# Loads in another order, w1 and w2 by halves of their columns: an attention and feed-forward kernel on one Trainium2 core

## The chip, the cores and the metric

The kernel runs on one core of a Trainium2 chip. The metric is the device time of one execution in microseconds. A core has several engines that run side by side, each through its own list of instructions in order: PE (the matmul engine, TensorE), DVE (VectorE), ACT (ScalarE), POOL (GpSimd) and SP (SyncE, which here only issues transfers). Transfers between the main memory and the core's SBUF are issued by SP or ACT (the hardware queues) or by POOL (the software queue) and are carried by 16 DMA engines. Matmuls write to PSUM, which here is one tile of eight banks; DVE or ACT must carry each result out of it.

## The reference

Attention with RMS-normalised q and k over 8 batches of 12 heads, 448 positions and 64 elements a head, and behind it a multiplicative feed-forward part on 3584 tokens of 768:

```python
def rmsnorm(x, g):
    rms = np.sqrt(np.mean(x * x, axis=-1, keepdims=True) + 1e-06)
    return x / rms * g
q_n, k_n = (rmsnorm(q, g_q), rmsnorm(k, g_k))
scores = 1.0 / np.sqrt(q.shape[-1]) * np.matmul(q_n, k_n.transpose(0, 1, 3, 2))
attn = softmax(scores)                      # over the last axis
x = np.matmul(attn, v)                      # then heads side by side: 3584 x 768
# feed-forward: w1, w2 768 x 1024; w3 1024 x 1024; w_out 1024 x 768
a = x @ w1
b = x @ w2
out = (a * b @ w3) @ w_out
```

All inputs and the output are float32. The kernel computes in bfloat16 with float32 sums.

## The kernel before

The work is cut into 24 quads: quad i holds four heads of one batch (three quads a batch). A quad passes through these steps:

1. **Load** of q and k (`load_qk`), 0.92 MB of float32, into one of three pairs of buffers, and of v (`load_v`), turned to bfloat16 on the way.
2. **Prep**: squares on ACT (`prep_sq`, L335), their sums on DVE (`prep_red`, L344), 1/rms on ACT as exp(-0.5 ln) (`prep_alpha`, L357 and L360), scaling on DVE (`prep_scale`, L376 to L390), and the transpose to the layout that the score matmuls need: on PE for the first five quads (L425), by a DMA transpose for the others (L402).
3. **Scores**: nine score units a quad, each eight matmuls (L457) into two banks and one exp on ACT (L471). Units go to PE in groups of three ("bursts", 24 matmuls).
4. **P x V**: three sets a quad, each 16 matmuls (L487): the sums of the rows with a matrix of ones, then the two halves of v. ACT makes 1/sum (L500, L502), DVE multiplies (L510) into xT.
5. When a batch's three quads are done, its **feed-forward** pieces go on a list of fillers (`push_ffn`): for each of eight column blocks x @ w1 (carried out to a_sb) and x @ w2 (multiplied by a_sb, L589), and the output matmuls of finished tokens (all on L523).

w3 @ w_out is computed first, on the core: each of the eight chunks of w3 is transposed on PE (L539), and 16 units of eight matmuls (L551) make w34 = w3 @ w_out, so that the feed-forward part ends with one product in place of two.

```python
    def w3_transpose(fc):
        ps, z = take(1)
        ...
        for gc in range(CF):
            nc.tensor.transpose(ps[:, gc, :], w3s[:, fc, gc * 128 : (gc + 1) * 128], ident)
        run("PE", 0.5)
        w3T_at[fc] = copy_out(z, w3T[:, :, fc * 128 : (fc + 1) * 128], ps, W_EV, CF * 128, True)

    def w34_unit(fc, nh):
        ...
        for gc in range(CF):
            nc.tensor.matmul(out=ps[:, 0:NH], lhsT=w3T[:, gc, fc * 128 : (fc + 1) * 128],
                             rhs=w_outs[:, gc, nh * NH : (nh + 1) * NH], ...)
        run("PE", 1.4)
        copy_out(z, w34s[:, fc, nh * NH : (nh + 1) * NH], ps[:, 0:NH], W_EV, NH)
```

The order of instructions on each engine is fixed when the program is built. The builder keeps a planned time for each engine (`clk`) with estimated costs, and a table of planned landing times (`LAND`); these planning values only decide an order, and nothing of them is in the program. In a first stage it takes, over and over, whatever PE can do first by the plan; where the plan sees a gap on PE it puts in matmuls on a constant tile (`warm`, L658), whose results are not read:

```python
        def choices():
            res = []
            m = burst_size()
            ...            # 0: a burst of score units; 1: a transpose of q and k
            ...            # 2: a P x V set
            if w34q:       # 3: the next of the w3 transposes and w3 x w_out units, in their order
                res.append((w34q[0][0](), 3, lambda: w34q.pop(0)[1]()))
            return res
        ...
        while w34q or not fillers:
            res = choices()
            ...
            x = min((x for x in res if x[0] <= now + 0.1), key=lambda x: x[1])
            gap = now - clk["PE"]
            if gap > 0.5 and now < 30:
                warm(int(gap * WARM_GAP / 0.22))
            clk["PE"] = now
            x[2]()
            try_load()
            try_v()
```

After it comes a steady stage, counted in score units: every third unit a burst of three, P x V sets at fixed distances from a quad's last burst (`KIND`), loads of q and k for quad n at unit 9 n + `LOAD_AT`, and the fillers spread over the rest. What remains of the fillers after the last quad is done at the end, with PE alone.

The loads of the first stage, in the old order:

```python
    LOADS = ["o0", "w0", "w1", "w2", "v0", "w3", "w4", "w5", "v1", "w6", "w7", "o1", "v2"]
    ...                    # o: a half of w_out's columns, w: a chunk of w3, v: a quad's v
        for t, part, eng, h0 in (             # quad 0, on SP's and ACT's queues
            (0, 0, nc.sync, 0), (1, 0, nc.scalar, 0), (1, 1, nc.sync, 0),
            (0, 0, nc.sync, 2), (1, 0, nc.scalar, 2), (1, 1, nc.scalar, 2),
        ):
            load_part(0, t, h0, 2, parts_of(0, t)[part], eng)
        ...
        load_qk(1)                            # on SP's queue
        load_qk(2)
        make_identity(nc, ident)
        if GATE is not None:                  # the software queue waits for quad 0's first q
            nc.gpsimd.tensor_copy(
                out=gate[0:NP0], in_=st[0][GATE[0]][0:NP0, GATE[1], 0, 0:1]
            )
        for x in LOADS:                       # on POOL's queue
            load_any(x)
        for h in range(HQ):
            for half in range(2):
                for w, src in ((w1s, moe_w1), (w2s, moe_w2)):
                    load_w12(w, src, h, half)
        load_v(3)
        warm(WARM)
```

Quads 3 and on are loaded on SP's queue as soon as their buffers may be written (`try_load`), on which the output's stores (L629) and the DMA transposes go as well.

## Time and profile before

| | |
|---|---|
| time, median of three runs | 378.12 us (378.03 to 378.63) |
| span of the profiled execution | 377.4 us |
| read from main memory, written to it | 46.66 MB, 11.01 MB |
| bytes moved by the DMA engines | 56.43 MB, mean 150 GB/s |
| score matmuls (L457) | 44.4 us of PE |
| P x V matmuls (L487) | 79.9 us of PE, four rows together |
| feed-forward matmuls (L523) | 245.5 us of PE, three rows together |
| w3 x w_out (L551) | 22.8 us of PE |

In a row of the groups stand the line, the engine and operation, what is written from what, the shape and the number; after the bar the busy time and the mean duration of one in ns, and after the second bar the time that the engine stood idle just before such instructions, with what ended it. A row of the waits has who waited for whom, the sum in us, how often, and the longest. A row of a timeline or of the chain starts with the start in us and the duration; consecutive instructions of one kind are one row. The window rows give the busy time and the number of instructions of each engine in a stretch, then the granted share of PE's clock, the busy share of the 16 DMA engines (as the trace counts it, it can read above 1) and the rate. Ends of matmuls are modelled, so neighbouring rows of PE can overlap by some tenths of a microsecond.

### The profile page before, as it was taken

The numbers are of one execution on the slowest core, as the hardware profiler recorded it, in microseconds if no ns is written. First come the engines' busy times: TensorE is split into PE (matmuls) and PEld (weight loads), VectorE is DVE, ScalarE is ACT, GpSimd is POOL, SyncE is SP. The second block draws the span as 40 slices with busy tenths as digits, with TensorE's granted clock in tenths as the row PEclk, the third lists the DMA queues.
The fourth block names the chain that finished last, engine by engine and source line by source line (L and its number), as shares of the span: only waits on it lengthen the run. The fifth ranks groups of instructions, "written<-read, shape, count | busy, mean of one in ns | idle before, by whom it ended". The sixth has DMA issues, their size and how long they took to land.

```text
span 377.4 us, 17123 instructions
## 1 busy us (share of the span) xinstructions
PE 364.8 (97%) x7677; PEld 197.7 (52%) x7678; DVE 239.9 (64%) x425; ACT 280.3 (74%) x472; POOL 76.6 (20%) x133
## 2 busy tenths in 40 slices
PE   5989999999999999999999998999999999999995
PEld 2346555555555565555555554555545555556563
DVE  5688898878676776687568656678668755321210
ACT  3779768889969888878798885988798887752222
POOL 7145454422022022022202211210201200000000
PEclk9899999999999999999999999999999999999999
DMA  8999999775989798958896989777996883004005
GB/s 178 236 232 230 226 215 215 92 142 118 195 180 167 151 147 177 213 81 187 159 197 107 157 184 180 158 120 161 196 176 86 199 150 61 2 20 113 2 20 152
DMA packets 92777, 56.43 MB, mean 150 GB/s; under 512 B 56928, under 2 KB 86688, under 8 KB 92704
## 3 DMA queue, kind: packets, MB, share of 16 engines
q1 hardware_dynamic: 70096, 42.45, 53.3%
q0 software_dynamic: 22016, 12.33, 24.4%
q8 instruction: 60, 0.98, 1.1%
q10 hardware_dynamic: 592, 0.56, 0.6%
q14 instruction: 13, 0.11, 0.1%
HBM read 46.66 MB, written 11.01 MB: 153 GB/s over the span
## 4 chain that ended last, share of the span: by engine, by line
PE 85%; DMA 8%; ACT 3%; SPq 1%; issue 1%; DVE 0%; ACTq 0%; DVEq 0%
PE banks_ps L523 54%; PE banks_ps L487 15%; PE banks_ps L457 9%; DMA k_sb<-in_k_dram 5%; PE banks_ps L551 5%; DMA q_sb<-in_q_dram 3%; ACT P L471 1%; PE banks_ps L425 1%; PE banks_ps L539 1%; ACT a_sb L203 1%; SPq L629 1%; SPq L254 1%; ACT sq L335 0%; ACT o_sb L203 0%; DVE o_sb L205 0%
## 5 line engine op out<-in xcount | busy, mean ns | idle before, releaser
L471 ACT ACTIVATE P<-banks_ps 128x896 bf16<-128x896 f32 x144 | 124.2, 922 | 14.0 <-PE banks_ps L457 13.7
L523 PE MATMUL banks_ps<-xT,w2s 128*32 128x448 bf16 x1536 | 83.8, 352 | 1.8 <-ACT a_sb L203 1.8
L523 PE MATMUL banks_ps<-xT,w1s 128*32 128x448 bf16 x1536 | 83.9, 353 | 0.0
L286 POOL DMA_DIRECT2D v_sb<-in_v_dram x72 | 43.8, 622 | 189.8 <-PE banks_ps L487 182.9
L523 PE MATMUL banks_ps<-w34s,abT 128*32 128x384 bf16 x1792 | 77.8, 326 | 0.0
L344 DVE TENSOR_REDUCE ssq<-sq 128x8 f32<-128x512 f32 (+1 forms) x96 | 63.5, 679 | 13.9 <-ACT sq L335 13.3
L589 DVE TENSOR_TENSOR abT<-banks_ps,a_sb 128x448 bf16<-128x448 f32 x64 | 39.8, 622 | 41.8 <-PE banks_ps L523 41.5
L523 PEld LDWEIGHTS <-abT 128*32 128x32 bf16 x1792 | 47.8, 97 | 26.5 <-DVE abT L589 0.3
L523 PEld LDWEIGHTS <-w2s 128*32 128x32 bf16 x1536 | 41.5, 97 | 33.4 <-issue 2.7
L523 PEld LDWEIGHTS <-w1s 128*32 128x32 bf16 x1536 | 40.8, 97 | 31.9 <-issue 2.2
L510 DVE TENSOR_TENSOR xT<-banks_ps,r 128x448 bf16<-128x448 f32 x48 | 29.6, 622 | 29.6 <-PE banks_ps L487 20.8
L203 ACT CAST a_sb<-banks_ps 128x448 bf16<-128x448 f32 x53 | 28.1, 530 | 25.9 <-PE banks_ps L523 25.1
L457 PE MATMUL banks_ps<-qkT 64*32 64x448 bf16 x1344 | 44.4, 357 | 0.7 <-DVE abT L589 0.3
L376 DVE TENSOR_TENSOR qtmp<-q_sb,alpha 128x512 bf16<-128x512 f32 (+1 forms) x48 | 33.0, 687 | 11.8 <-ACT alpha L360 10.3
L203 ACT COPY o_sb<-banks_ps 128x384 f32<-128x384 f32 x42 | 20.1, 478 | 23.1 <-PE banks_ps L523 23.0
L487 PE MATMUL banks_ps<-P,v_sb 128*32 128x448 bf16 x576 | 35.8, 354 | 0.0
L335 ACT ACTIVATE sq<-q_sb 128x512 f32<-128x512 f32 (+1 forms) x48 | 30.0, 625 | 5.6 <-DMA q_sb<-in_q_dram 5.6
L390 DVE TENSOR_TENSOR qks<-k_sb,alpha 128x512 bf16<-128x512 f32 x48 | 32.8, 684 | 0.6 <-ACT alpha L360 0.6
L335 ACT ACTIVATE sq<-k_sb 128x512 f32<-128x512 f32 x48 | 30.1, 628 | 3.2 <-DMA k_sb<-in_k_dram 3.2
L487 PEld LDWEIGHTS <-v_sb 128*32 128x32 bf16 x768 | 18.9, 96 | 18.7 <-issue 6.9
L457 PEld LDWEIGHTS <-qkT 64*32 64x32 bf16 x1344 | 15.1, 90 | 25.9 <-issue 21.0
L471 ACT ACTIVATE Pr<-banks_ps 128x896 bf16<-128x896 f32 x24 | 22.1, 920 | 2.2 <-PE banks_ps L457 2.2
(53 smaller groups left out, 265.3 us busy)
## 6 DMA issues: line engine op xcount, KB each, us to landing
out_dram<-o_sb SPq DMA_DIRECT2D x48, 192.0 KB, 2.9
k_sb<-in_k_dram SPq DMA_DIRECT2D x23, 256.0 KB, 5.9
q_sb<-in_q_dram SPq DMA_DIRECT2D x21, 256.0 KB, 4.7
k_sb<-in_k_dram SPq DMA_DIRECT2D x23, 192.0 KB, 5.7
q_sb<-in_q_dram SPq DMA_DIRECT2D x21, 192.0 KB, 5.0
v_sb<-in_v_dram POOLq DMA_DIRECT2D x24, 96.0 KB, 3.4
w3s<-in_moe_w_dram POOLq DMA_DIRECT2D x8, 256.0 KB, 10.6
w_outs<-in_moe_w_out_dram POOLq DMA_DIRECT2D x4, 384.0 KB, 10.8
```

The costliest lines, as they stand in the source:

```text
L203: nc.scalar.copy(out=out, in_=in_)
L286: nc.gpsimd.dma_start(out=dst.rearrange("p h j d -> p h (j d)"), in_=part.rearrange("p h j d -> p h (j d)"),)
L335: nc.scalar.activation(out=s["sq", pr][0:n, t], in_=(s["q"], s["k"])[t][0:n, 2 * pr : 2 * pr + 2], func=AF.Square,)
L344: nc.vector.tensor_reduce(out=s["ssq"][0:n, t, 2 * pr : 2 * pr + 2, :], in_=s["sq", pr][0:n, t], axis=AX, op=ADD,)
L376: nc.vector.tensor_tensor(out=s["qtmp"][0:n].transpose([0, 2, 1, 3]), in0=s["q"][0:n, hs], in1=alpha[0:n, 0, hs].unsqueeze(3).broadcast_to ...
L390: nc.vector.tensor_tensor(out=s["qks", pr][:, 1].transpose([0, 2, 1, 3]), in0=s["k"][:, hs], in1=alpha[:, 1, hs].unsqueeze(3).broadcast_to ...
L457: nc.tensor.matmul(out=sc[c0 : c0 + 32, u, 0:S], lhsT=qkT[u * D : (u + 1) * D, pr, 1, k0 : k0 + 32], rhs=qkT[u * D : (u + 1) * D, pr, 0, 0:S],
L471: lambda: nc.scalar.activation(out=dst, in_=sc[:, :, 0:S], func=AF.Exp),
L487: nc.tensor.matmul(out=ps[h * HALF : (h + 1) * HALF, :], lhsT=w, rhs=s["P"][:, h, j, :] if j < NF else s["Pr"][:, h % 2, :], start=(j == 0 ...
L510: lambda e: nc.vector.tensor_tensor(out=xT[b][:, 2 * m + kind - 1, :], in0=ps, in1=s["r"], op=MULT),
L523: nc.tensor.matmul(out=ps[32 * h : 32 * h + 32, 0:n], lhsT=lhsT[:, 32 * h : 32 * h + 32], rhs=rhs, start=start, stop=stop, tile_position=( ...
L589: lambda e: nc.vector.tensor_tensor(out=abT[bp][:, fi, odd * S : (odd + 1) * S], in0=ps[:, 0:S], in1=a_sb, op=MULT,),
```

## The change

w1 and w2 are loaded in two halves of their columns, for all rows, in place of slices of 32 partitions with all columns, so that the first column blocks of the feed-forward part need only the first half; the first stage may now take feed-forward pieces as well, and runs until the second half is planned to have landed. Quads 1 and 2 leave SP's queue and stand in the list of the software queue, among the weights, in the order in which they are meant to be needed; the gate at that queue's head is gone. Loads of later quads are placed 6 score units earlier (`LOAD_AT` from -17 to -23). The planning constants and the landing table are set anew.

```diff
--- before.py
+++ after.py
@@ -52,32 +52,33 @@
     O_BUFS = 3
     F_BUFS = 3
     G = 3
-    KIND = (3, 4, 6)
+    KIND = (2, 4, 6)
     N_PE_T = 5
     N_SQ_ACT = 24
-    A_EV = "AD"
-    O_EV = "AD"
-    W_EV = "DA"
-    BIAS = 0.2
-    SLACK = (0.3, 0.3)
-    EXP_SLACK = 0.6
+    A_EV = 'AD'
+    O_EV = 'AD'
+    W_EV = 'DA'
+    BIAS = 0.6
+    SLACK = (0.5, 0.2)
+    EXP_SLACK = 1.05
     WARM = 16
-    WARM_GAP = 0.6
-    PACE = 0.8
-    SLACK_0 = (2,1)
+    WARM_GAP = 0.3
+    PACE = 1.1
+    SLACK_0 = (2.4, 0.6)
     URGE = 0.3
-    AHEAD = 0
-    LAG = 8
+    AHEAD = 0.0
+    LAG = 7
     UNITS = 1.45
-    V_COST = 0.65
-    V_AHEAD = 5
-    LOAD_AT = -17
-    LATE = 6
-    T0 = 9.0
-    LOADS = ["o0", "w0", "w1", "w2", "v0", "w3", "w4", "w5", "v1", "w6", "w7", "o1", "v2"]
-    GATE = ("q", 0)
-    QK_AFTER = (0, 0)
-    LAND = {'o0': 18.8, 'o1': 40.8, 'w0': 20.5, 'w1': 22.2, 'w2': 23.9, 'v0': 25.7, 'w3': 27.4, 'w4': 29.099999999999998, 'w5': 30.799999999999997, 'v1': 32.599999999999994, 'w6': 34.3, 'w7': 36.0, 'v2': 42.599999999999994, 'q1': 9.7, 'q2': 14.7, 'q3': 27, 'q4': 37, 'q5': 47, 'v3': 60, 'w12': 58}
+    V_COST = 0.75
+    V_AHEAD = 13
+    LOAD_AT = -23
+    LATE = 7
+    T0 = 8.0
+    LOADS = ['q1', 'w0', 'w1', 'o0', 'w2', 'v0', 'q2', 'w3', 'w4', 'w5', 'w6', 'v1', 'w7', 'o1', 'v2', 'x0', 'v3', 'x1']
+    GATE = None
+    GATE_T = {1: 13.0, 2: 13.0}
+    AVAIL = 16.0
+    LAND = {'g': 5.6, 'q1': 10.4, 'w0': 11.6, 'w1': 12.9, 'o0': 18.4, 'w2': 20.1, 'v0': 23.8, 'q2': 27.0, 'w3': 28.6, 'w4': 30.3, 'w5': 32.0, 'w6': 33.6, 'v1': 37.2, 'w7': 38.5, 'o1': 45.2, 'v2': 48.1, 'x0': 57.5, 'v3': 61.3, 'x1': 71.3, 'q3': 23.9, 'q4': 37.0, 'q5': 52.5, 'q6': 69.6}
 
     const = ctx.enter_context(tc.tile_pool(name="const", bufs=1))
     load_pool = ctx.enter_context(tc.tile_pool(name="load", bufs=3))
@@ -260,14 +261,14 @@
             ),
         )
 
-    def load_qk(i):
+    def load_qk(i, eng=None):
         s = st[i]
         s["q"], s["k"] = qk_bufs[i % 3]
         if 3 <= i < 6:
             nc.vector.memset(s["q"][NP - 32 : NP, :, NF, :], 0.0)
         for t in range(2):
             for part in parts_of(i // NQB, t):
-                load_part(i, t, 0, HQ, part, nc.sync)
+                load_part(i, t, 0, HQ, part, eng or nc.sync)
 
 
 
@@ -289,14 +290,13 @@
             )
         nc.gpsimd.dma_start(out=s["v"][REST:NP, 2:4, NF], in_=lo[:, 2:4, NF])
 
-    def load_w12(dst, src, h, half):
-        issued.add(("w12", h, half))
-        nc.gpsimd.dma_start(
-            out=dst[h * HALF : (h + 1) * HALF, half::2, :],
-            in_=src.rearrange(
-                "(s h a d) f -> h a d s f", s=NQB, h=HQ, a=2, d=HALF
-            )[h, half],
-        )
+
+    def load_w12(half):
+        f = slice(half * DFF // 2, (half + 1) * DFF // 2)
+        for dst, src in ((w1s, moe_w1), (w2s, moe_w2)):
+            rows = src.rearrange("(s h a d) f -> s a h d f", s=NQB, h=HQ, a=2, d=HALF)
+            for c in range(CM):
+                nc.gpsimd.dma_start(out=dst[:, c, f], in_=rows[c // 2, c % 2, :, :, f])
 
     def load_w3(c):
         issued.add(("w3", c))
@@ -321,6 +321,10 @@
             load_wout(a, 1)
         elif kind == "w":
             load_w3(a)
+        elif kind == "x":
+            load_w12(a)
+        elif kind == "q":
+            load_qk(a, nc.gpsimd)
         else:
             load_v(a)
 
@@ -637,17 +641,18 @@
 
     def push_ffn(b):
         for fi in range(CF):
-            fillers.append(lambda b=b, fi=fi: ffn1_a(b, fi))
-            fillers.append(lambda b=b, fi=fi: ffn1_b(b, fi))
+            key = "x%d" % (2 * fi // CF)
+            fillers.append((key, lambda b=b, fi=fi: ffn1_a(b, fi)))
+            fillers.append((key, lambda b=b, fi=fi: ffn1_b(b, fi)))
         bp, odd = divmod(b, 2)
         for t in range(3, 7) if odd else range(3):
             for nh in range(2):
-                fillers.append(lambda bp=bp, t=t, nh=nh: ffn2(bp, t, nh))
+                fillers.append(("", lambda bp=bp, t=t, nh=nh: ffn2(bp, t, nh)))
 
     def fill(n):
         for _ in range(n):
             if fillers:
-                fillers.pop(0)()
+                fillers.pop(0)[1]()
 
     def warm(n):
         if not n:
@@ -694,13 +699,20 @@
                 add("t", pr, "SP", 0.0, lambda pr=pr: prep_dma_transpose(n, pr), x)
         chains.append(dict(n=n, avail=avail, ops=ops))
 
-    next_load = [3]
-
-    def try_load():
+    next_load = [next(n for n in (1, 2, 3) if "q%d" % n not in LOADS)]
+
+    def try_load(now=None):
         n = next_load[0]
+        if n < 3:
+            if now is None:
+                now = clk["DVE"]
+            if now < GATE_T[n]:
+                return
+            if GATE_T[n]:
+                nc.vector.memset(qk_bufs[n][0][0:1, 0, 0, 0:1], 0.0)
         if n < NQ and all(c["n"] > n - 3 for c in chains):
             load_qk(n)
-            push_prep(n, LAND.get("q%d" % n, clk["PE"] + 6.0))
+            push_prep(n, LAND.get("q%d" % n, clk["PE"] + AVAIL))
             next_load[0] += 1
 
     next_v = [4]
@@ -733,8 +745,11 @@
         nc.vector.memset(ones[0:REST, 2], 0.0)
         for t_sb in v_bufs:
             nc.vector.memset(t_sb[:, :, NF, :], 0.0)
-        load_qk(1)
-        load_qk(2)
+        push_prep(0, 7.0, (1,))
+        for n in range(1, next_load[0]):
+            push_prep(n, LAND["q%d" % n])
+        try_load(0.0)
+        try_load(0.0)
         make_identity(nc, ident)
         if GATE is not None:
             nc.gpsimd.tensor_copy(
@@ -742,17 +757,14 @@
             )
         for x in LOADS:
             load_any(x)
-        for h in range(HQ):
-            for half in range(2):
-                for w, src in ((w1s, moe_w1), (w2s, moe_w2)):
-                    load_w12(w, src, h, half)
-        load_v(3)
         warm(WARM)
 
         for t in range(2):
             prep_sq(0, 0, t)
         for t in range(2):
             prep_red(0, 0, t)
+        try_load(7.0)
+        try_load(7.0)
         prep_alpha(0, 0, 2)
         prep_scale(0, 0, 2)
         prep_scale(0, 0, 0)
@@ -768,9 +780,8 @@
         for e in clk:
             clk[e] = T0
         prep_pe_transpose(0, 0)
-        push_prep(0, 7.0, (1,))
-        push_prep(1, LAND["q1"])
-        push_prep(2, LAND["q2"])
+        try_load(9.5)
+        try_load(9.5)
 
         w34q = []
         add_t = lambda fc: w34q.append(
@@ -827,6 +838,8 @@
                 res.append((t, 2, lambda: pv_set(i, kind)))
             if w34q:
                 res.append((w34q[0][0](), 3, lambda: w34q.pop(0)[1]()))
+            if fillers and len(w3T_at) == CF and (fillers[0][0] or not w34q):
+                res.append((LAND.get(fillers[0][0], 0.0), 4, lambda: fill(1)))
             return res
 
         def burst(m):
@@ -834,7 +847,7 @@
             for _ in range(m):
                 qk_exp(units[0])
 
-        while w34q or not fillers:
+        while w34q or not fillers or clk["PE"] < LAND["x1"]:
             res = choices()
             now = min([max(clk["PE"], x[0]) for x in res] or [clk["PE"] + 0.3])
             while True:
```

## The prediction

> **What bounds the kernel now.** I read the page's first two parts, then the groups of instructions by line, then the waits, the windows of the first 30 us, PE's own timeline up to the first feed-forward matmul, and last the chain of work around 230 us.
>
> ```profile
> PE 364.8 (97%) x7677; PEld 197.7 (52%) x7678; DVE 239.9 (64%) x425; ACT 280.3 (74%) x472; POOL 76.6 (20%) x133
> ```
>
> PE, the matmul engine, is busy for 364.8 of 377.4 us. But part of that does nothing for the result. The groups by line and the waits show what:
>
> ```profile
> L658 PE MATMUL banks_ps<-warm_t 128*128 128x512 bf16 x44 | 12.9, 449 | 1.5 <-DVE warm_t L725 1.2 <-issue 0.3
> ...
> PE banks_ps L765 <- DVE gp_row L759: 3.0, 1, 3.0
> PE banks_ps L523 <- ACT a_sb L203: 1.8, 2, 1.6
> ```
>
> Line 658 is warming: matmuls whose result nobody reads, 12.9 us. PE's last matmul ends at about 373.4 us (the last row of the chain of waits starts at 343.53 and lasts 29.89). So PE stands idle for 373.4 - 364.8 = 8.6 us before its end, and 8.6 + 12.9 = 21.5 us of the span carry no useful matmul. Only 1.8 us of these lie late, on the second wait above. The other 19.7 us lie at the start, where the windows show this:
>
> ```profile
> 10.00:14.00 4.00, 3.57 (x38) 1.45 (x40) 2.13 (x5) 3.10 (x5) 0.00 (x0) 0.69 1.22 235
> 14.00:18.00 4.00, 3.90 (x22) 1.73 (x21) 2.50 (x5) 3.88 (x10) 0.65 (x2) 0.88 1.18 245
> 18.00:22.00 4.00, 3.95 (x46) 2.01 (x43) 3.83 (x9) 1.56 (x5) 1.61 (x3) 1.00 1.15 234
> 22.00:26.00 4.00, 2.92 (x38) 1.67 (x29) 3.20 (x7) 3.44 (x6) 1.83 (x3) 1.00 1.23 229
> 26.00:30.00 4.00, 4.00 (x59) 2.46 (x57) 3.71 (x8) 3.57 (x5) 1.72 (x3) 1.00 1.14 235
> ```
>
> The last three columns are the granted clock, the DMA share and GB/s. DMA is full (share 1.14 to 1.23, 229 to 245 GB/s) in every window: the start is bound by what has landed. PE's timeline says when it has work at last:
>
> ```profile
> 19.62 0.61 PE L539 MATMUL banks_ps<-ident,w3s 128*128 128x128 bf16 x8
> ...
> 22.72 1.48 PE L551 MATMUL banks_ps<-w_outs,w3T 128*128 128x384 bf16 x8
> ...
> 28.83 0.62 PE L539 MATMUL banks_ps<-ident,w3s 128*128 128x128 bf16 x8
> ...
> 65.98 0.37 PE L523 MATMUL banks_ps<-xT,w1s 128*32 128x448 bf16 x4
> ```
>
> The first chunk of w3 is transposed at 19.6 us, the first w3 x w_out unit (L551) starts at 22.7, and from about 28.8 PE has no gap until the feed-forward part begins at 65.98.
>
> The late 1.8 us are seen in the chain near 230 us:
>
> ```profile
> 226.56 0.56 DVE o_sb L205
> ...
> 227.13 0.47 SPq L629
> ...
> 228.29 0.67 SPq L254
> ...
> 229.00 5.94 DMA q_sb<-in_q_dram
> ...
> 235.02 0.16 ACT sq L335
> ...
> 235.56 0.52 ACT a_sb L203
> ...
> 236.12 1.32 PE banks_ps L523 x24
> ```
>
> SyncE issues in order: an output store (L629) waits for its evacuation, the load of q (L254) stands behind it, lands at 234.9, ACT stands at the square of q (L335), and the a_sb copy that PE's next group needs stands behind the square. PE waits 1.64 us there; at 154 us the same chain costs it 0.17 us.
>
> **What the Trainium skill says.** "Perfetto Trace Analysis", section Identifying the Most-Contended Engine, warns that matmul busy time is no measure of the distance to the limit. This trace agrees: 12.9 of the 364.8 us are warming. "DMA: Bandwidth & Descriptors", section Issuing engines are not separate DMA queues, says that transfers issued by different engines run on the same 16 DMA engines and interleave. The windows agree: the total stays near 235 GB/s while both queues have work, so quads 1 and 2 on SyncE's queue take bandwidth from the weights. The same page, Specifications, asks for at least 512 B a descriptor; halves of w1 and w2 read 2,048 B and write 1,024 B a row, still above, and no run here has shown such rows yet. "TensorE: Matmul & The Clock Gate", section What's actually happening, says that the clock is halved until PE has been busy for some 3.4 us. The trace agrees in kind: 0.69 granted in 10 to 14 us, and the first burst of 24 score matmuls takes 1.32 us against 0.76 later.
>
> **Part 1, the order of the loads.** Before, quads 1 and 2 (0.92 MB each) go out at once on SyncE's queue beside w_out's first half, and w3 follows. After, one queue carries quad 1, w3 chunks 0 and 1, w_out's first half, w3 chunk 2, v0, quad 2, w3 chunk 3 and so on. Up to chunk 3 the bytes are the same set in both, and DMA is full in both, so I do not expect chunk 3 sooner than before (28.83 in the timeline; the changed kernel's own landing table, a planning value, has 28.6). What changes is how much PE can do before it: two transposes of w3 at about 12 us, not 20, the first w3 x w_out unit at about 18.4, not 22.7 (again the table), and all of quad 0's P x V, which before starts at 33.2 us.
>
> I list PE's instruction order in both kernels and price it with the old trace, start to start: a w3 transpose group 0.46 us, a w3 x w_out unit 1.30, a burst of 24 score matmuls 0.69, a transpose set of q and k 0.65 (quads 1, 2) or 0.80 (quad 3 on), a P x V set of 16 matmuls 0.77.
> Before, from 28.83 to 65.98: 5 x 0.46 + 14 x 1.30 + 6 x 0.69 + 2 x 0.65 + 4 x 0.80 + 9 x 0.77 = 36.1 us; the trace says 37.15, so the sum is 3% short.
> After, from the fourth w3 transpose to the first feed-forward matmul: 5 x 0.46 + 14 x 1.30 + 6 x 0.69 + 2 x 0.65 + 2 x 0.80 + 6 x 0.77 = 32.2 us, with 3% 33.1. From 28.6 that is 61.7 us.
> At that point the new order still owes what the old one has done by then: two score units (0.46 us) and two transpose sets (1.6 us), 2.1 us. Equal work is reached at 63.8 us, not 65.98: a gain of 2.2 us. Fewer warming matmuls (26, not 45) gain nothing in themselves; they fill waits.
>
> **Part 2, w1 and w2 by halves of their columns.** 16 transfers of 192 KB become 24 of 128 KB. In the old trace one takes GpSimd 0.56 us to issue, so 8 more are 4.5 us of GpSimd, beside PE's work. The use: the first half of the feed-forward columns may start when half the bytes are there. The table has them at 57.5 and 71.3 us. PE needs the first at 61.7; the second only after four column pairs, 8 x 1.135 = 9.1 us of matmuls, with bursts, transposes and a P x V set between, some 14 us, so at about 76. Slack of 4 and 5 us: worth 0 by itself, but it lets feed-forward start before all weights are there, which part 1 needs.
>
> **Part 3, loads 6 score units earlier.** From 66 to 377 us 141 units are left, 2.2 us each, so 6 units are 13 us. The late q came 3 us too late for ACT. The load also goes ahead of the stores that held it up. Both waits should go: 1.8 us.
>
> **Part 4, the other constants** (slacks, the first P x V set one unit earlier, evacuation bias). PE's steady stretch has nothing left to win but those 1.8 us, so they can only lose; I allow 0.5 us.
>
> Sum: -2.2 - 1.8 + 0.5 = -3.5 us: 378.1 becomes 374.6 us.
>
> **The rivals.**
> (a) The start is filled entirely. The 19.7 us hold about 10 us before the first scores that no load order removes, so at most some 8 us are to be had, with part 3 near 369 us. Against it: DMA is already full, and the bytes ahead of chunk 3 are the same.
> (b) A new wait on a load. PE's order is fixed: a score burst now stands behind the second w3 transpose, and w3 x w_out units behind w_out's second half, for which the table leaves nothing (45.2 us, PE there at about 45). Each microsecond that a transfer is late is one more in the end. In the old trace w1 and w2 transfers took 8.5 us to land; if the small ones took as long with eight in flight, they would run at 123 GB/s and the slack would be gone. That makes 376 to 380 us.
> (c) New waits in the steady stretch. P x V one unit earlier may meet exponentials that ACT (74% busy) has not done; 0.3 us for each of 21 quads would be 6 us, 380. For it speaks only that PE follows others closely; against it, that two units are 4.4 us of PE and three exponentials 2.8 us of ACT.
> (d) The clock drops with less warming. A few tenths up to 2 us, in the start alone, where arrivals bind anyway.
>
> **Range and chances.** (a) in part gives 371.5, (b) or (c) in part 378.3. Over 2% faster needs 370.6 us, nearly all of (a); over 2% slower needs 385.7, (b) and (c) together.
>
> **What would show it.** Right: first w3 transpose near 12 us, first feed-forward matmul near 62, no wait of ACT on q above 1 us late, warming below 10 us. Wrong: PE waits on w3, w_out, w1 or w2 after 29 us; feed-forward after 64 us; or PE idle over 2 us in the steady stretch.

## The result and the profile after

| | before | after |
|---|---|---|
| time, median of four runs each | 378.16 us (378.03 to 378.63) | 384.26 us (382.45 to 385.30) |
| span of the profiled execution | 377.4 us | 382.0 us |
| ratio after / before | | 1.0154, interval 1.0113 to 1.0195 |

The changed kernel is 1.5% slower. The prediction was 374.6 us, in a range up to 378.3. The profiled executions took 379.94 us before, which is above the range in the table, and 383.81 us after; so their spans lie 4.6 us apart and the medians 6.1. The lines below are those of the changed kernel's profile; its line numbers are four higher (L527 for the old L523, and so on).

The page, the busy times and two of the DMA queues (packets, MB, share of 16 engines):

```profile
PE 364.2 (95%) x7657; PEld 196.9 (52%) x7659; DVE 234.3 (61%) x416; ACT 282.4 (74%) x481; POOL 86.7 (23%) x146
...
q0 software_dynamic: 33440, 14.20, 29.5%
q8 instruction: 60, 0.98, 1.1%
```

PE's busy time has hardly moved (364.8 before), so the time came mostly as idle time of PE. The software queue had 22,016 packets before and has 33,440 now. The line below it, which looked like nothing before, will matter: the queue that brings the engines their own instructions.

PE's timeline at the four places that the prediction named:

```profile
12.43 0.92 PE L543 MATMUL banks_ps<-ident,w3s 128*128 128x128 bf16 x8
...
18.20 1.46 PE L555 MATMUL banks_ps<-w_outs,w3T 128*128 128x384 bf16 x8
...
28.88 0.62 PE L543 MATMUL banks_ps<-ident,w3s 128*128 128x128 bf16 x8 [1.70 <-DMA w3s<-in_moe_w_dram]
...
62.24 1.32 PE L527 MATMUL banks_ps<-xT,w1s 128*32 128x448 bf16 x24
```

Up to here it went as planned: first transpose of w3 at 12.4 us, first w3 x w_out unit at 18.2, feed-forward from 62.2 in place of 65.98. The bracket is the idle time just before: PE did wait 1.7 us for w3's fourth chunk. The late waits near 154 and 230 us are gone too, as the windows of the second half show (length, then PE's busy time). Before:

```profile
150.00:230.00 80.00, 79.41 (x1836) 42.95 (x1828) 54.95 (x94) 66.88 (x114) 14.54 (x24) 1.00 0.87 161
230.00:310.00 80.00, 78.23 (x1808) 42.30 (x1800) 54.90 (x95) 65.99 (x112) 12.12 (x20) 1.00 0.85 157
```

After:

```profile
150.00:230.00 80.00, 80.00 (x1864) 42.68 (x1860) 53.78 (x92) 69.50 (x118) 14.29 (x24) 1.00 0.92 163
230.00:310.00 80.00, 80.00 (x1864) 44.12 (x1855) 53.92 (x92) 69.36 (x119) 14.31 (x24) 1.00 0.82 153
```

So both ends are better, and the middle must have cost more than both brought. PE's waits name it:

```profile
PE banks_ps L527 <- issue: 4.3, 3, 3.6
...
PE banks_ps L491 <- issue: 1.5, 1, 1.5
```

5.8 us (5.9 with more digits) of waits on "issue", which means that no semaphore, no buffer and no data explains them. All four lie between 74 and 98 us. The chain of work in that stretch (start, duration, what), from the second of them to the fourth:

```profile
81.62 0.39 issue
82.01 3.20 PE banks_ps L527 x62
85.21 0.69 PE banks_ps L461 x24
85.90 2.19 PE banks_ps L527 x42
88.09 0.39 issue
88.48 0.55 PE banks_ps L527 x6
89.03 0.76 PE banks_ps L491 x16
89.79 0.69 PE banks_ps L461 x24
90.48 1.25 PE banks_ps L527 x24
91.73 0.76 PE banks_ps L491 x16
92.48 2.00 PE banks_ps L527 x42
94.49 3.57 issue
98.06 1.17 PE banks_ps L527 x14
```

Count the matmuls between the stops: 62 + 24 + 42 = 128, and 6 + 16 + 24 + 24 + 16 + 42 = 128. Each matmul has its weight load, so PE stops exactly every 256 instructions, in the middle of a group whose data was there. From the first stop (74.01) to the second it is 128 matmuls again. Now the page's instruction queue: 0.98 MB in 60 packets is 16.3 KB a packet; 0.98 MB over PE's 7,657 + 7,659 instructions is 64 B each; so one packet holds 256 instructions. PE stopped because the next piece of its own program had not arrived. "Runtime: NRT & Kernel Launch" in the Trainium skill, section Instruction fetch mechanics, has the same number (blocks of 16 KiB, 256 instructions, fetched over a DMA queue of the sequencer's own while the block before runs), and calls the cost "mostly hidden". The trace agrees with the 256; in this stretch the cost wasn't hidden.

When the packets came can be read from half-microsecond windows of the DMA view. Before, they start at 63.0, 67.5, 73.5, 80.5, 85.0, 91.0 and 97.0 us: 5.7 us apart on average. After, at 72.0, 79.5, 86.0 and 95.0: 7.7 us apart, up to 9. Each takes 1.0 to 1.4 us, and PE goes on 1.0 to 2.1 us after its end: the one of 95.0 has a share of 16.2% of 16 engines' 0.5 us, 1.3 us, so it ends by 96.8, and PE starts at 98.06.

A second cost follows the longest stop. The windows around it (the third number from the end is PE's granted clock):

```profile
96.00:98.00 2.00, 0.00 (x0) 0.00 (x0) 0.57 (x1) 0.00 (x0) 0.00 (x0) 1.00 1.44 117
98.00:100.00 2.00, 1.94 (x38) 0.68 (x38) 0.00 (x0) 0.67 (x2) 0.00 (x0) 0.60 1.15 248
100.00:102.00 2.00, 2.00 (x36) 0.72 (x24) 0.00 (x0) 1.76 (x3) 0.00 (x0) 0.55 1.12 223
```

Behind the 3.57 us without work the clock falls. The 0.60 and 0.55 are means over windows that lie partly outside; from 98.5 to 101.5 us it is 0.50. 14 feed-forward matmuls take 1.17 us in place of 0.57, a burst of scores 1.25 in place of 0.69, and the P x V set behind it 1.54 in place of 0.87. That is 1.8 us more. 5.9 + 1.8 = 7.7 us, and 382.0 - 7.7 = 374.3: by this sum the changed kernel would be faster than the old one without the stops.

### The profile page after: what moved, and what is told of

The parts are those of the page before. It is cut to its first block, busy times and chain, and to the rows that moved or that the text cites. A ratio compares the mean times of both kernels' runs of the same rounds, so it can differ in the third digit from the quotient of the medians.

```text
span 382.0 us, 17064 instructions
## 1 busy us (share of the span) xinstructions
PE 364.2 (95%) x7657; PEld 196.9 (52%) x7659; DVE 234.3 (61%) x416; ACT 282.4 (74%) x481; POOL 86.7 (23%) x146
## 3 DMA queue, kind: packets, MB, share of 16 engines
q0 software_dynamic: 33440, 14.20, 29.5%
## 4 chain that ended last, share of the span: by engine, by line
PE 89%; DMA 6%; issue 2%; POOL 2%; DVE 0%; ACT 0%; POOLq 0%
PE banks_ps L527 58%; PE banks_ps L491 15%; PE banks_ps L461 10%; DMA w3s<-in_moe_w_dram 6%; PE banks_ps L555 5%; PE banks_ps L429 1%; PE banks_ps L543 1%; POOL w_outs L310 0%; POOL k_sb L255 0%; POOL w3s L303 0%; POOL q_sb L255 0%; DVE qks L394 0%; POOL g_row L736 0%; POOL g_row L735 0%; ACT o_sb L204 0%
## 5 line engine op out<-in xcount | busy, mean ns | idle before, releaser
L475 ACT ACTIVATE P<-banks_ps 128x896 bf16<-128x896 f32 x144 | 125.5, 924 | 10.1 <-PE banks_ps L461 9.7
L527 PE MATMUL banks_ps<-xT,w2s 128*32 128x448 bf16 x1536 | 85.0, 353 | 0.8 <-issue 0.8
L527 PE MATMUL banks_ps<-xT,w1s 128*32 128x448 bf16 x1536 | 84.5, 353 | 0.0
L527 PE MATMUL banks_ps<-w34s,abT 128*32 128x384 bf16 x1792 | 80.4, 327 | 3.6 <-issue 3.6
L348 DVE TENSOR_REDUCE ssq<-sq 128x8 f32<-128x512 f32 (+1 forms) x96 | 62.7, 680 | 10.9 <-ACT sq L339 10.4
L527 PEld LDWEIGHTS <-abT 128*32 128x32 bf16 x1792 | 47.9, 97 | 31.8 <-issue 6.6
L527 PEld LDWEIGHTS <-w2s 128*32 128x32 bf16 x1536 | 40.8, 97 | 34.3 <-issue 5.4
L527 PEld LDWEIGHTS <-w1s 128*32 128x32 bf16 x1536 | 40.8, 97 | 33.3 <-issue 4.8
L204 ACT CAST a_sb<-banks_ps 128x448 bf16<-128x448 f32 x62 | 33.1, 534 | 32.9 <-PE banks_ps L527 32.5
L204 ACT COPY o_sb<-banks_ps 128x384 f32<-128x384 f32 x47 | 22.6, 481 | 25.8 <-PE banks_ps L527 25.0
L491 PE MATMUL banks_ps<-P,v_sb 128*32 128x448 bf16 x576 | 36.9, 358 | 1.5 <-issue 1.5
L339 ACT ACTIVATE sq<-k_sb 128x512 f32<-128x512 f32 x48 | 30.6, 638 | 3.0 <-DMA k_sb<-in_k_dram 3.0
L461 PEld LDWEIGHTS <-qkT 64*32 64x32 bf16 x1344 | 14.8, 90 | 24.3 <-issue 19.9
```

Of the source, the lines that this page charges most:

```text
L204: nc.scalar.copy(out=out, in_=in_)
L339: nc.scalar.activation(out=s["sq", pr][0:n, t], in_=(s["q"], s["k"])[t][0:n, 2 * pr : 2 * pr + 2], func=AF.Square,)
L348: nc.vector.tensor_reduce(out=s["ssq"][0:n, t, 2 * pr : 2 * pr + 2, :], in_=s["sq", pr][0:n, t], axis=AX, op=ADD,)
L461: nc.tensor.matmul(out=sc[c0 : c0 + 32, u, 0:S], lhsT=qkT[u * D : (u + 1) * D, pr, 1, k0 : k0 + 32], rhs=qkT[u * D : (u + 1) * D, pr, 0, 0:S],
L475: lambda: nc.scalar.activation(out=dst, in_=sc[:, :, 0:S], func=AF.Exp),
L491: nc.tensor.matmul(out=ps[h * HALF : (h + 1) * HALF, :], lhsT=w, rhs=s["P"][:, h, j, :] if j < NF else s["Pr"][:, h % 2, :], start=(j == 0 ...
```

## The experiments

What kept the packets back? In that stretch the transfers of w1 and w2 are still under way. The DMA view of the changed kernel, 37 to 80 us (first the queue's packets, MB and share; then for each transfer its number, size and microseconds from issue to landing):

```profile
q0 software_dynamic: 15169, 4.42, 86.6%
...
w1s<-in_moe_w_dram POOLq DMA_DIRECT2D x12, 128.0 KB, 8.9
w2s<-in_moe_w_dram POOLq DMA_DIRECT2D x12, 128.0 KB, 10.5
...
qkT<-qks SPq DMA_TRANSPOSE x1, 10.7
```

Each piece of w1 or w2 now goes to 128 partitions from rows that lie in four runs of 32, because the rearrangement puts (h, d) side by side where the tensor has h, a, d. The last piece is issued at 71.18 us (54.77 before), so the loading of weights, and of the v behind them, reaches into the DMA transposes that begin at 74.48.

Theory A: the form of these pieces makes them slow and is the cause. Its rivals: the loads placed 6 units earlier crowd the queues (B), or the new order and constants around them do it (C). All ratios are against executions of the kernel before that were taken beside those of the run.

**e1: the same halves, cut as before into slices of 32 partitions.** The order, the constants and the rest of the change stay.

```diff
-            rows = src.rearrange("(s h a d) f -> s a h d f", ...)
-            for c in range(CM):
-                nc.gpsimd.dma_start(out=dst[:, c, f], in_=rows[c // 2, c % 2, :, :, f])
+            rows = src.rearrange("(s h a d) f -> h a d s f", ...)
+            for h in range(HQ):
+                for a in range(2):
+                    nc.gpsimd.dma_start(out=dst[h * HALF : (h + 1) * HALF, a::2, f], in_=rows[h, a][:, :, f])
```

> The changed kernel with w1 and w2 still by halves of their columns, but each half in 16 slices of 32 partitions by three rows (96 KB each) in place of 12 blocks of 128 partitions (128 KB each); rows stay 1,024 bytes, PE's order is the same. Theory A (the shape of the pieces slows the DMA engines from 40 to 82 us, the loads of v pile up behind, and PE's own instructions arrive late): the 4-byte packets fall from 11,456 to some 2,400, the last piece of w1/w2 lands some 8 us sooner, PE's waits with the cause issue after 70 us fall from 5.9 us to under 1, time 374 to 377 us. Rival B (it is the loads of q and k placed 6 units earlier): waits and time stay, 382 to 385 us. Rival C (it is that half rows are small, whatever their shape): some 380 us or more.

Measured: 376.62 us, ratio 0.9933 (0.9916 to 0.9951). No wait on issue after the start. 24,352 packets on the software queue; pieces of w1 and w2 land in 5.6 and 5.0 us. 384.26 became 376.62 by the form of the w1 and w2 transfers alone: the loss needs this form. B and C by themselves, which e1 keeps, don't make it.

**e2: whole rows of w1 and w2, the old transfers, at the place of the first half.**

```diff
     def load_w12(half):
+        if half:
+            return
+        # the 16 old transfers of 192 KB, all columns
```

> The changed kernel with w1 and w2 loaded as before (16 slices of 32 partitions with all 1,024 columns, 2,048-byte rows), all of them at the place of the first half. Theory A and rival C: waits of PE with the cause issue after 70 us under 1 us, time 374 to 377 us, with perhaps a wait for weights at the first feed-forward matmuls near 62 us of up to 2 us, since nothing can start on a half. Rival B: 382 to 385 us.

Measured: 377.33 us, 0.9955 (0.9939 to 0.9971), no wait on issue. The halves as such aren't needed for the repair, nor do they bring much: e1 is 0.7 us ahead, with intervals that overlap.

**e3: the kernel before with nothing but the new pieces.**

```diff
-        # 16 transfers of 192 KB
+        load_w12(0)
+        load_w12(1)      # as in the changed kernel: 24 pieces of 128 KB
```

> The kernel before with only the new shape of the w1/w2 loads (24 blocks of 128 partitions by half the columns), all else and PE's order as before. Theory A: the loads of w1 and w2 end some 8 to 10 us later than before, near 72 us, so PE first waits for w1/w2 at 66 us by up to 5 us, and then has waits with the cause issue of its own; 382 to 388 us. Rival B: no change beyond the wait for the weights, under 380 us.

Measured: 385.42 us, 1.0169 (1.0133 to 1.0206): as large a loss without any other part of the change. But PE doesn't wait for w1 or w2, as theory A expected it to, and only 1.58 us are an instruction stop (at 85.82). More shows up later:

```profile
240.57 1.78 PE L521 MATMUL banks_ps<-xT,w2s 128*32 128x448 bf16 x24 [2.84 <-ACT a_sb L203]
```

That is the old late wait on q, 1.64 us before, now 2.84, and behind it the clock at 0.83 from 240 to 250 us, 1.7 us more. ACT waits 8.0 us for q in all (5.6 before). Stops, the larger late wait and the clock make 1.6 + 1.2 + 1.7 = 4.5 of the 6.6 us between the spans. PE's order is that of the kernel before, so the two can be matched instruction by instruction: the rest is lost in small pieces, 0.6 us between 72 and 82 us, 0.3 around the stop, 1.0 between 113 and 122, 0.1 near 160, and 0.5 behind PE's last matmul, less 0.4 gained at the start. What delays q isn't shown.

**e4: the changed kernel with the loads back at -17.**

```diff
-    LOAD_AT = -23
+    LOAD_AT = -17
```

> The changed kernel with the loads of q and k back at 17 units ahead, PE's order the same. Theory A: the waits with the cause issue between 70 and 100 us stay within 2 us of 5.9, and late waits for q come back (some 1 to 2 us in all): 383 to 387 us. Rival B: the waits between 70 and 100 us go, 376 to 379 us.

Measured: 386.38 us, 1.0216 (1.0161 to 1.0271), slower still. On the time B falls. On the stops it doesn't:

```profile
81.90 0.93 PE L527 MATMUL banks_ps<-xT,w2s 128*32 128x448 bf16 x14 [0.39 <-issue]
```

That stop of 0.39 us is all that is left of 5.9 us, where A expected little change and B none left. So in this kernel the stops need the earlier loads as well as the slow pieces. The time is lost elsewhere: from 110 to 370 us PE is idle for 5.6 us in small waits, 4.6 of them on ACT, of which the changed kernel has none. With the new constants the earlier loads are needed more, not less.

**f1: the same blocks of 128 partitions by 512 columns, but from 128 rows in line.** The rows of w1 and w2 are not sorted into the order of x's columns, which this kernel leaves out; bytes, pieces and order are those of the changed kernel.

```diff
-            rows = src.rearrange("(s h a d) f -> s a h d f", ...)
+            rows = src.rearrange("(c p) f -> c p f", p=128)
             for c in range(CM):
-                nc.gpsimd.dma_start(out=dst[:, c, f], in_=rows[c // 2, c % 2, :, :, f])
+                nc.gpsimd.dma_start(out=dst[:, c, f], in_=rows[c, :, f])
```

> The changed kernel with the same 24 blocks of 128 partitions by 512 columns, 1,024-byte rows, but each block from 128 rows that follow one another in w1 or w2 (one run of rows, not 4 runs of 32). The rows of w1 and w2 so stand in another order than the computation needs, so the output isn't the reference's; sizes, number of transfers and PE's order are the same. Theory A1 (the source in 4 runs of 32 rows makes the transfer poor: 384 extra 4-byte packets each and few DMA engines): packets of the software queue fall from 33,440 to some 24,200, a w1/w2 transfer lands in 5 to 7 us and not 9 to 10, PE's waits with the cause issue after 70 us under 1 us, time 374 to 377 us. Rival A2 (half rows in blocks of 128 partitions are poor whatever their source): 382 to 385 us as the changed kernel.

Measured: 377.12 us, 0.9958 (0.9943 to 0.9974), no wait on issue after the start. The same DMA view:

```profile
q0 software_dynamic: 8035, 5.10, 82.6%
...
w1s<-in_moe_w_dram POOLq DMA_DIRECT2D x12, 128.0 KB, 5.7
w2s<-in_moe_w_dram POOLq DMA_DIRECT2D x12, 128.0 KB, 7.4
...
qkT<-qks SPq DMA_TRANSPOSE x1, 3.1
```

This is the cleanest comparison: number, size and row length of the pieces are equal, only the source's shape differs. Over the whole run the software queue has 24,224 packets against 33,440: 9,216 fewer, 384 for each of the 24 pieces. Their bytes (14.20 against 14.17 MB) make them some 4 B each. "DMA: Bandwidth & Descriptors", section Why a DMA increments its semaphore by 16 and not by 1, says how many DMA engines share a transfer: the largest number up to 16 that divides the slowest dimension of both sides. An estimate by that rule is 4 for a source of 4 x 32 rows and 16 for 128 rows; the 384 packets would then be 32 for each of 12 engines left out. The page also names exceptions on the software queue, and the trace doesn't tell engines apart, so neither is seen here. What is seen is 8.9 and 10.5 us to landing in place of 5.7 and 7.4.

PE's order is the same in the changed kernel, e1, e2, e4 and f1, so two score bursts can be followed through them. In the changed kernel (start, duration):

```profile
72.58 0.76 PE L461 MATMUL banks_ps<-qkT 64*32 64x448 bf16 x24
...
105.31 0.76 PE L461 MATMUL banks_ps<-qkT 64*32 64x448 bf16 x24
```

and in f1:

```profile
75.26 0.76 PE L461 MATMUL banks_ps<-qkT 64*32 64x448 bf16 x24
...
99.13 0.76 PE L461 MATMUL banks_ps<-qkT 64*32 64x448 bf16 x24
```

From the one to the other PE takes 32.7 us in the changed kernel, 23.9 in f1 and in e2, 24.3 in e1 and 24.8 in e4. So the stretch costs 8.9 us against f1: the 7.7 counted above, and 1.2 in delays that the profile doesn't show as stops. Ahead of it the changed kernel had been 2.7 us earlier than f1.

The same match tells in what way the packets are late. Blocks of 256 instructions begin at 75.54, 82.01, 88.48 and 98.06 us in the changed kernel; in f1 the same blocks begin at 76.35, 82.07, 87.79 and 93.47 us. The next packet starts 4.1, 4.1, 6.7 and 4.1 us after these moments in the changed kernel, and 0.2, 0.6, 1.1 and 1.6 us in f1. Once started it takes 1.0 to 1.3 us in both. So the packets aren't slow on the way; they start late. How far they are apart says less: in e1 two start 9.6 us apart, at 65.2 and 74.8 us, and PE doesn't stop.

**f2 and f3: the kernel before with spare traffic.** After the sixth v it also loads 1.6 MB of w1 and w2 (as bfloat16) into a tile that nobody reads: in f2 as 12 pieces of the slow form, in f3 as 16 slices of the good form. The question is whether the form alone, away from the weights' order, makes the stops.

```diff
+        if i == 5:
+            spare()      # f2: 12 blocks from 4 x 32 rows; f3: 16 slices of 32 partitions
```

> The kernel before, with 12 added transfers behind the load of v for quad 5 (about 84 us), of the changed kernel's shape (128 partitions from 4 runs of 32 rows, 512 columns), into a spare tile that nobody reads; the output is the reference's and PE's order is as before. Theory A (PE's own instructions come by the same DMA engines and arrive late while such transfers are under way): PE waits with the cause issue between 84 and 105 us, 1 to 6 us in all, and 380 to 384 us. Rival D (the waits that the trace calls issue are really waits for w1, w2 or v): PE depends on none of this, so no such waits, 378 us within 0.7.

> As the run with spare blocks, but the same bytes in 16 slices of 32 partitions by three rows. Theory A: under 0.5 us of waits with the cause issue after 84 us, 378 to 379.5 us. If it is only the added bytes that count, it is as slow as the spare blocks.

Measured: f2 391.08 us, 1.0341 (1.0286 to 1.0396), with 5.7 us of waits on issue and one of 4.0 us for a DMA transpose; f3 383.67 us, 1.0146 (1.0108 to 1.0184). The extra loads ran earlier than I had meant, at some 67 to 83 us. In f2 the stops are as A has them, the time is worse than the 380 to 384 us expected. f3 is not as A has it: slices of the good form, and yet its chain has

```profile
84.66 3.13 issue
87.79 0.75 PE banks_ps L501 x11
...
93.87 0.46 issue
94.33 0.75 PE banks_ps L501 x11
```

with instruction packets at 67.0, 76.0 and 85.0 us, 9 apart. So a stop doesn't need the slow form; 1.6 MB more in the good form can make one too. What f2, f3 and the changed kernel have in common is that DMA transposes on SyncE's queue are slow. From issue to landing, those issued between 37 and 80 us take 10.7 us in the changed kernel and 3.1 in f1 (the views above), 3.7 in e1, 3.1 in g1 (below), and in f3

```profile
qkT<-qks SPq DMA_TRANSPOSE x2, 8.9
```

That gives theory T: the instruction packets are late where DMA transposes meet much traffic of the software queue; the slow form counts because it stretches that traffic into the transposes. SyncE's timeline (start, duration, number) sets T a limit at once. In the changed kernel the first two transposes are

```profile
74.48 7.27 SPq L406 DMA_TRANSPOSE qkT<-qks  x2
```

and the first stop has begun before them, at 74.01: that stop isn't theirs. In f3

```profile
70.19 4.40 SPq L416 DMA_TRANSPOSE qkT<-qks  x2
...
84.90 8.65 SPq L416 DMA_TRANSPOSE qkT<-qks  x2
```

the stop at 84.66 comes just before the second pair, and the first pair has landed by 83.5. A slow transpose may also be one more thing that the same traffic holds up, and not a cause.

**g1: the kernel before with the loads 6 units earlier, and nothing else.** This is not on the stops, but on part 3 of the prediction.

```diff
-    LOAD_AT = -17
+    LOAD_AT = -23
```

> The kernel before with only the loads of q and k moved from 17 to 23 units ahead, PE's order the same. The prediction's part 3: the late wait of 1.6 us near 235 us goes, and that near 154 us, so 376.3 us (375.8 to 377.0). If the loads wait for their buffers anyway: 378 us.

Measured: 376.38 us, 0.9955 (0.9938 to 0.9972); the spans differ by 377.4 - 375.2 = 2.2 us. The windows of its second half:

```profile
150.00:230.00 80.00, 79.58 (x1844) 42.88 (x1836) 55.28 (x96) 67.47 (x114) 14.53 (x24) 1.00 0.87 163
230.00:310.00 80.00, 79.87 (x1852) 42.81 (x1848) 56.33 (x97) 67.58 (x114) 12.12 (x20) 1.00 0.84 149
```

PE idles 0.55 us in these 160, before 2.4 (79.41 and 78.23 busy, shown above).

**h1, h2 and g2: the wait for w3's fourth chunk.** e1 and e2 start feed-forward at 65.54 and 64.43 us, not at 62.24 (each from one profiled execution; e1's is the slowest of 20, 378.86 us). In e1 PE's timeline and the windows say why:

```profile
30.62 0.62 PE L546 MATMUL banks_ps<-ident,w3s 128*128 128x128 bf16 x8 [2.21 <-DMA w3s<-in_moe_w_dram]
```
```profile
30.00:34.00 4.00, 3.38 (x40) 1.61 (x40) 2.62 (x5) 1.48 (x4) 1.86 (x3) 0.70 1.15 237
```

That is a wait of 2.2 us, and a mean clock of 0.70 behind it (0.50 from 31.8 to 34.8 us). h1 is e1, and h2 is e2, with eight matmuls on the constant tile ahead of that transpose; g2 is e1 with that chunk ahead of quad 2.

```diff
     def w3_transpose(fc):
+        if fc == 3:
+            warm(8)                                  # h1, h2
-    LOADS = [..., 'v0', 'q2', 'w3', 'w4', ...]
+    LOADS = [..., 'v0', 'w3', 'q2', 'w4', ...]       # g2, with its planned landings
```

> The run with w1 and w2 in slices of 32 partitions (376.62 us), with 8 more warming matmuls placed on PE ahead of the fourth w3 transpose, where PE waited 2.2 us for the chunk and then ran at a granted clock of 0.70 in 30 to 34 us. Theory P (the new order of the loads gains 2 us, and the fall of the clock behind this wait eats it): clock 0.95 or more in 30 to 38 us, first feed-forward matmul at 62.5 to 63.5 us (65.5 without), and 374.0 to 375.2 us. Rival: the clock falls anyway or the weights come no sooner, 376 to 377 us.

> The same 8 warming matmuls in the run with w1 and w2 in whole rows (377.33 us). Theory P: clock 0.95 or more in 30 to 38 us, first feed-forward matmul at 62 to 63 us (64.4 without), and 374.5 to 375.7 us. Rival: 376.5 to 377.5 us.

> The run with w1 and w2 in slices of 32 partitions, with the fourth chunk of w3 loaded ahead of quad 2 in place of behind it (0.92 MB sooner, some 3.9 us at 235 GB/s), and the landing table changed with it, so that PE's order takes the transpose sooner. Theory P: PE's wait for that chunk near 29 us falls under 1 us, the clock stays at 0.95 or more in 26 to 34 us, 374 to 375.5 us. If quad 2's q and k are then missed instead, PE has a wait for qks or qkT between 30 and 40 us and the time stays at 376 to 378 us.

Measured: h1 375.95 us, 0.9935 (0.9914 to 0.9956), and h2 376.37, 0.9950 (0.9931 to 0.9969), in both the clock at full in this stretch and feed-forward from 63.2 us; g2 376.92, 0.9961 (0.9947 to 0.9975). Neither h1 nor h2 reached its expected range. h1 is the lowest median of all, but its ratio is e1's: that the warming helps isn't shown. In g2 the wait only moved on to the next chunk (2.19 us, up to 31.23), so the order of these two loads decides nothing.

The length of such a wait doesn't decide whether the clock falls. The changed kernel, e1, e2, e4, f1 and k1 have the same loads up to there, and in their profiles PE waits 1.70, 2.21, 2.27, 1.68, 2.43 and 1.23 us for this chunk. Behind it the clock is 0.50 for some 3.4 us in all but the first (worked out from 0.57 over four microseconds in e2). It stays at 1.00 behind g2's 2.19 us, and behind the 3.13 us of f3's stop. What decides it, these runs don't show. In e1's 20 executions time and mean clock go together: the five at 0.985 or 0.986 took 376.67 to 377.70 us, the seven at 0.993 to 0.995 took 374.64 to 376.03.

**k1: theory T from the other side.** The changed kernel, slow pieces and all, but with quads 5 to 7 transposed on PE, so that no DMA transpose falls into the stretch. It costs PE six sets of 0.81 us, 4.9 us.

```diff
-    N_PE_T = 5
+    N_PE_T = 8
```

> The changed kernel, its poor w1/w2 blocks kept, with the q and k of quads 5, 6 and 7 transposed on PE (6 sets of 0.8 us, 4.8 us more of PE) and not by DMA, so that no DMA transpose is under way while w1, w2 and the v behind them are loaded; PE's order changes with it. If the late arrival of PE's instructions needs DMA transposes beside the software queue's transfers (theory T): PE's waits with the cause issue after 70 us fall from 5.9 us to under 1, and the time is 381 to 383.5 us in spite of the added PE work. If the blocks alone are enough: waits of 3 us or more stay, 386 us or more.

Measured: 383.23 us, 1.0116 (1.0084 to 1.0149). Of the instruction stops one is left, 0.80 us at 75.05, and the packets come 5 us apart on average from 79.5 to 95.0. From 70 to 110 us PE idles 1.5 us, in the changed kernel 5.9. So with 4.9 us more to do it is no slower, as T expected. T is still argued and not shown. The run changes PE's order, too; the stop that stays is the one that T couldn't explain, and the packet behind it starts 4.1 us after its block begins (79.9 and 75.85 us), as in the changed kernel, with no transpose on the way; the next one starts 2.7 us in. And e4, with four transposes in a row beside the same slow pieces (15.0 us of SyncE's queue from 76.11 on), has 0.4 us of stops.

## Why the prediction was wrong

The result lies 6 us above the upper end of the range, on the slower side.

- **Part 2, "worth 0 by itself", is the step that failed.** I priced the new transfers by GpSimd's issue time and by the length of their rows (1,024 B and more, "still above" 512). What changed was neither: the source's shape, four runs of 32 rows, gave each piece 384 more packets and 8.9 to 10.5 us to landing where the same block in line takes 5.7 to 7.4. Beside them PE's instruction packets started 4.1 to 6.7 us into a block, and PE waited for its own instructions: 5.9 us, then 1.8 us of clock, and 1.2 us in smaller delays. Instead of 0 the term was about +8.9 us (the changed kernel against f1). It took the earlier loads of part 3 as well: at -17 the same pieces cost 0.9 us in the same stretch (e4 against f1). The prediction took its parts one by one and had no term for two of them together.
- **The rivals.** (b) was near: it named slow w1 and w2 transfers, but took the old landing time of 8.5 us for eight in flight and looked for a wait of PE on the weights. There is none; the weights came in time, and what came late was something I had on no list. The working had "PE idle over 2 us in the steady stretch" as a sign that it would be wrong, and that is what the trace has, for a cause that it didn't name. (c) didn't happen: PE is busy for all of 150 to 310 us. (d) happened in the changed kernel behind the longest stop, and at the start, where it was looked for, in the profiles of e1, e2, e4, f1 and k1: half the clock for some 3.4 us, worth 1.7 us. In the profiles of h1 and h2, with eight warming matmuls more, it isn't there. (a) didn't happen.
- **Part 3 was right, size too.** Expected -1.8 us; g1 gives 0.45% of 378.3, -1.7 us.
- **Part 1 was right in its places, and too large.** Transposes, w3 x w_out units and the first feed-forward matmul of the changed kernel came within 0.6 us of what was worked out (12.4, 18.2, 62.2 against 12, 18.4, 61.7). But with the repaired form the first three parts and the constants give 0.9933 to 0.9958 (e1, e2, f1, h1, h2), of which g1 has 0.9955 alone: what remains for parts 1 and 4 is 0 to -0.8 us, no more than the intervals' width, and not -2.2 + 0.5. The mis-sized term is the landing of w3's fourth chunk: 28.6 us from the planning table, but its transpose starts at 28.3 to 30.6 us in the six profiles with the same loads up to there, behind waits of 1.2 to 2.4 us, and in five of the six the clock falls behind it.
- **Part 4's 0.5 us** wasn't measured by itself. With the slow pieces and the loads at -17 PE is idle from 110 to 370 us for 5.6 us with the new constants (e4) and for 4.2 with the old ones (e3). No run has this pair without the slow pieces.
- **The sum.** Without the 8.9 us the profiled execution would have taken 383.81 - 8.9 = 374.9 us, and the prediction would have been 0.3 us too low for it. The repaired kernels (375.95 to 377.33) lie 1.4 to 2.7 us above the prediction; so the 0.3 is in part luck of one execution in which the clock didn't fall at the start.

What stays open: why the instruction packets start late, that is, on which engine and behind what they wait, which the trace doesn't show; what it takes besides much traffic of the software queue (f3 has a stop without the slow pieces, e4 and k1 have little of it with them); what makes the clock fall behind a wait; and why the changed kernel's own executions lie as far apart as 382.45 and 385.30.

The version to keep is e1: halves of the columns in slices of 32 partitions, 376.62 us, 0.7% faster than the kernel before and 2.0% faster than the change as made (376.62 / 384.26 = 0.980). Most of that is the earlier loads: g1, the kernel before with one constant changed, is 0.5% faster, and the two intervals overlap.

## What to carry to other kernels

When a load is cut anew, look at the shape of both sides of each transfer, not at its bytes and its row length alone: a source in a few runs, here 4 x 32 rows, took half as long again to land as the same block in line. When PE stops for "issue" in the middle of a group, count the instructions between the stops; 256 each time, or 128 matmuls with their weight loads, meant here that its program was fetched too late, and what helped was to change the transfers of that moment, their form (e1, f1) or their time (e4). And a time saved at the start can be lost by what the loads then meet: compare when each queue is done, not only when the first user gets its data.

## What the runs showed of the hardware that I had not expected

- PE's instructions come in packets of 16 KB on a DMA queue that takes 1.1% of the DMA engines' time, some 5.7 us of PE's work each in the kernel before from 63 to 97 us, and this supply can be late: packets that start 4.1 to 6.7 us after the block ahead of them, where f1 has 0.2 to 1.6, and stops of 0.4 to 3.6 us.
- A piece of 128 KB from 4 x 32 rows has 384 packets of about 4 B more than one from 128 rows in line, and lands in 8.9 and 10.5 us, not 5.7 and 7.4 (7.6 and 9.5 in e4, 7.6 and 10.7 in k1).
- Two DMA transposes took 4.0 to 4.2 us of SyncE's queue in the kernel before, and up to 8.65 us beside more traffic of the software queue, even with slices of the good form (f3).
- PE's clock fell to 0.50 for some 3.4 us behind waits of 1.2 to 2.4 us (k1, e4, e1, e2, f1) and of 3.6 us (the changed kernel), but not behind waits of 1.7 (the changed kernel), 2.2 (g2) and 3.1 us (f3).
